# A fused dynamic convolution, rational MLP and SwiGLU kernel: weight decode and bounds moved, the convolution's taps laid innermost, a fixed order of work

## Chip, cores and metric

The kernel runs on one core of a Trainium2 chip. The metric is the device time of one execution in microseconds (us); lower is better. PE is TensorE, DVE VectorE, ACT ScalarE, POOL GpSimd, SP SyncE (which only issues DMAs here).

## What is computed

The input x has 2 x 4096 tokens of 192 channels, treated as 8192 tokens. Three layers follow one another; cut to what matters:

```python
w = softmax(weight_gen, axis=-1)                    # per token: 8 heads x 7 taps, 1e-09 added to the sum
x = einsum('bshk,bskhg->bshg', w, x_unf)            # causal window of 7 tokens, 24 channels per head
h = x @ w_in                                        # 192 -> 2048
P = a[0] + a[1] * h + a[2] * h2 + a[3] * h3
Q = 1.0 + np.abs(b[0]) * np.abs(h) + np.abs(b[1]) * h2
x = (P / (Q + 1e-6)) @ w_out                        # 2048 -> 192
xn = x / rms * rms_g
silu = g * (1.0 / (1.0 + np.exp(-g)))               # g = xn @ w_gate, 192 -> 1536
out = silu * (xn @ w_val) @ w_out                   # 1536 -> 192, a second w_out
```

The four weight matrices arrive as float64, everything else as float32.

## The kernel before

**Tiling.** A partition holds 64 tokens in a row. The work is cut into 32 blocks of 256 tokens (two per partition). In a block the 2048 hidden columns of the first MLP are four quads of 512, so there are 128 quads; the 1536 columns of the second are two halves of 768.

**A block.** The softmax over the taps (jobs "s", some for two or four blocks at once) runs on DVE, POOL and ACT. POOL multiplies x with each of the seven taps (L352, tile pt, taps outermost); the sum over taps is a reduction on DVE with a strided read (L361) or, for the first six blocks, six additions on POOL (L367, the rule ADDP). ACT takes the fp16 part (L371), POOL the rest (L375), and a transposing DMA on SP makes xt (L380). mm1 is, for each quad, four groups of five fp16 matmuls (L767) of the split weights w1A, w1B and w1C into the PSUM tile h, of which there are two. The rational function of a quad is then a chain over the engines: ACT squares h into tB (L777) and takes its scaled magnitude into tA (L781); DVE makes Q in tA ("q", L784); ACT takes logarithm and exponential of it, 1/Q in tC (L788, L791); DVE makes P in h (p1 and p2, L795, L799) and the fp16 product g1h (L804); ACT adds a constant to Q (qc, L807), POOL multiplies it with g1h (m, L810), DVE subtracts (d, L813) and POOL makes the fp16 rest g1l (L817). d is the last to read h, and so what frees it for the quad two further on. mm2 (L833 to L835) multiplies g1h and g1l with the split w_out into acc, of which there is one buffer. The RMS norm runs on ACT and POOL; its fp16 parts xn are written by ACT (L872) and POOL (L876), and a transposing DMA makes xnT (L881). mm3 makes gate and val (L767) in the PSUM tile gv, a single buffer; ACT's silu (L907) frees it for val, DVE's product (L912) for the next gate. mm4 (L921) multiplies in float32 with the second w_out, ACT copies out (L927) and SP stores.

**Weights.** Each of 20 pieces of the float64 weights is decoded to float32. ACT makes a mask in SBUF in three operations (L423, L425, L426: square, sign, relu), DVE assembles the bits in three (L445, L451, L454), all on SBUF. Then bounds are taken that set powers of two as scales: ACT squares each piece (L469), for w_in PE sums the squares with a matrix of ones (L472) into gv, and allmax (L155, L156) takes the maximum over partitions with a transpose on PE into gv. ACT and either POOL (L497) or DVE (L499) split each piece into fp16 parts.

**What sets the order.** Every operation is a job with an engine, a cost, its dependencies and the buffers that it takes. order() gives each job a due time, from the list TIMES for the first blocks and for the rest from a period T_SLOT of 9.8432 per quad and the offsets OFF, and a list scheduler in the kernel then writes the program, engine by engine. Each engine works its queue in order. All DMAs are on SP's queue.

## Time and profile before

| what | value |
|---|---|
| device time, median of 3 runs | 1412.8 us |
| lowest and highest | 1411.08 and 1414.57 us |
| the profiled execution: its span | 1411.8 us |
| another time of that execution | none is given; the span is used as its own time |
| PE busy | 1241.5 us, 88% |
| DVE busy | 1200.8 us, 85% |
| ACT busy | 1153.9 us, 82% |
| POOL busy | 1044.7 us, 74% |
| DMA, mean | 38 GB/s |

The busy times are of the whole span. Matmul records are pipelined and overlap, so a matmul's own mean is not what it adds to the time; the distance from one start to the next is.

### The profile page before, as it was taken

What the parts mean: (1) busy time and instruction counts of PE and PEld (TensorE: products, weight loads), DVE (VectorE), ACT (ScalarE), POOL (GpSimd) and SP (SyncE); (2) the same over time, 40 slices, a digit from 0 to 9 for tenths busy, and PEclk for the clock granted to TensorE, in tenths of its full rate; (3) what the DMA queues carried; (4) which work ended last, traced back from release to release, by engine and by line L of the source; (5) the groups of instructions that cost most, each with busy time, mean ns of one, the idle gap of its engine ahead of it and who ended that gap; (6) DMA issues with size and microseconds to landing.
All of it is one profiled execution on the core that took longest, in us unless ns stands there. A gap on an engine that the chain in (4) does not pass through costs nothing.

```text
span 1411.8 us, 26479 instructions
## 1 busy us (share of the span) xinstructions
PE 1241.5 (88%) x11026; PEld 1134.7 (80%) x11026; DVE 1200.8 (85%) x1018; ACT 1153.9 (82%) x1410; POOL 1044.7 (74%) x874
## 2 busy tenths in 40 slices
PE   1313488999999999999999999999999999999998
PEld 0212378889889988888889898898889898999997
DVE  5999998888988888888899888888888988888741
ACT  5777877888888888888888888888888888888862
POOL 2977797988777777788777777777877777777540
PEclk9657799999999999999999999999999999999999
DMA  7432233100100020000200010001000000000000
GB/s 200 143 96 70 57 85 78 51 22 18 58 15 16 12 61 18 21 18 18 61 18 16 15 57 13 21 18 60 18 18 21 13 21 13 15 16 18 18 12 18
DMA packets 70664, 54.19 MB, mean 38 GB/s; under 512 B 54034, under 2 KB 66194, under 8 KB 69648
## 3 DMA queue, kind: packets, MB, share of 16 engines
q1 hardware_dynamic: 70544, 52.51, 14.0%
q8 instruction: 86, 1.41, 0.4%
q14 instruction: 34, 0.28, 0.1%
HBM read 31.26 MB, written 6.29 MB: 27 GB/s over the span
## 4 chain that ended last, share of the span: by engine, by line
PE 37%; DVE 16%; ACT 14%; POOL 13%; issue 5%; DMA 4%; POOLq 0%; DVEq 0%; ACTq 0%
PE gv L767 15%; PE h L767 9%; PE acc L921 6%; POOL g1l L817 6%; DMA xnT<-xn 4%; DVE tA L784 3%; DVE g1h L804 3%; DVE h L799 3%; POOL tA L810 3%; POOL xn L876 2%; DVE gp L912 2%; ACT tC L791 2%; ACT tC L788 2%; ACT tA L807 2%; PE acc L835 2%
## 5 line engine op out<-in xcount | busy, mean ns | idle before, releaser
L810 POOL TENSOR_TENSOR tA<-tA,g1h 128x1024 f32<-128x1024 f32 x128 | 276.6, 2161 | 194.5 <-DVE g1h L804 174.0
L817 POOL TENSOR_TENSOR g1l<-tA,tC 128x1024 f16<-128x1024 f32 x128 | 306.8, 2409 | 52.7 <-DVE tA L813 32.5
L767 PE MATMUL h<-xt,w1A 128*128 128x256 f16 x1024 | 220.8, 278 | 86.4 <-DVE tA L813 68.2
L921 PE MATMUL acc<-wo,gp 128*128 128x192 f32 x1464 | 252.3, 327 | 1.5 <-ACT osb L927 1.4
L833 PE MATMUL acc<-wo1h,g1h 128*128 128x192 f16 x1008 | 248.0, 246 | 0.4 <-ACT y L840 0.4
L834 PE MATMUL acc<-wo1l,g1h 128*128 128x192 f16 x1008 | 248.0, 246 | 0.0
L835 PE MATMUL acc<-wo1h,g1l 128*128 128x192 f16 x1008 | 248.0, 246 | 0.0
L352 POOL TENSOR_TENSOR pt<-xc,wg 128x384 f32<-128x384 f32 x224 | 241.9, 1105 | 1.8
L921 PEld LDWEIGHTS acc<-wo,gp 128*128 128x128 f32 x1464 | 236.8, 191 | 3.0 <-ACT osb L927 1.7
L784 DVE SCALAR_TENSOR_TENSOR tA<-tB,cf,tA 128x1024 f32<-128x1024 f32 x128 | 201.8, 1577 | 32.9 <-ACT tA L781 32.9
L777 ACT ACTIVATE tB<-h 128x1024 f32<-128x1024 f32 x128 | 130.5, 1020 | 90.2 <-PE h L767 90.2
L767 PE MATMUL h<-xt,w1C 128*128 128x256 f16 x1024 | 200.2, 278 | 0.0
L813 DVE SCALAR_TENSOR_TENSOR tA<-h,cf,tA 128x1024 f32<-128x1024 f32 x128 | 163.7, 1279 | 41.8 <-POOL tA L810 41.8
L767 PE MATMUL gv<-xnT,w3gA 128*128 128x256 f16 x756 | 164.7, 275 | 33.1 <-DMA xnT<-xn 29.1
L795 DVE SCALAR_TENSOR_TENSOR h<-tB,cf,h 128x1024 f32<-128x1024 f32 x128 | 163.5, 1279 | 34.4 <-ACT tA L781 31.3
L767 PEld LDWEIGHTS <-w1A 128*128 128x128 f16 x1024 | 102.0, 100 | 95.9 <-DVE tA L813 42.6
L767 PE MATMUL gv<-xnT,w3vA 128*128 128x256 f16 x768 | 170.2, 273 | 6.1 <-ACT gp L907 6.1
L804 DVE SCALAR_TENSOR_TENSOR g1h<-h,cf,tC 128x1024 f16<-128x1024 f32 x128 | 163.6, 1278 | 12.0 <-ACT tC L791 3.4
L781 ACT ACTIVATE tA<-h,cf 128x1024 f32<-128x1024 f32 x128 | 142.0, 1110 | 35.2 <-PE h L767 19.1
L799 DVE SCALAR_TENSOR_TENSOR h<-tB,cf,h 128x1024 f32<-128x1024 f32 x128 | 163.9, 1281 | 1.3
L788 ACT ACTIVATE tC<-tA,cf 128x1024 f32<-128x1024 f32 x128 | 146.5, 1145 | 20.7 <-DVE tA L784 19.9
L912 DVE SCALAR_TENSOR_TENSOR gp<-gp,val_s,gv 128x1536 f32<-128x1536 f32 x64 | 115.8, 1810 | 51.5 <-PE gv L767 51.0
(215 smaller groups left out, 2844.4 us busy)
## 6 DMA issues: line engine op xcount, KB each, us to landing
xc<-in_x_dram SPq DMA_DIRECT2D x7, 1344.0 KB, 6.6
...
```

Of the source, the lines that this page charges most:

```text
L352: nc.gpsimd.tensor_tensor(out=pt_t[b][:, k].rearrange("p i (h g) -> p i h g", h=NH), in0=xc_t[k0][:, o0 + k:o0 + k + 2, :].rearrange("p i ...
L767: nc.tensor.matmul(out=dst, lhsT=w[:, fs], rhs=xt[:, :, c, :], start=(n == 0), stop=(n == 4))
L784: nc.vector.scalar_tensor_tensor(out=tA[q], in0=tB[q], scalar=cfb(q)[:, 1:2], in1=tA[q], op0=ALU.mult, op1=ALU.add)
L788: nc.scalar.activation(out=tC[q], in_=tA[q], func=ACTF.Ln, scale=float(2.0 ** -LNS), bias=cfb(q)[:, 8:9])
L799: nc.vector.scalar_tensor_tensor(out=h, in0=tB[q], scalar=cf[:, 5:6], in1=h, op0=ALU.mult, op1=ALU.add)
L804: nc.vector.scalar_tensor_tensor(out=g1h[q], in0=hps[q], scalar=cf[:, 3:4], in1=tC[q], op0=ALU.add, op1=ALU.mult)
L810: nc.gpsimd.tensor_tensor(out=tA[q], in0=tA[q], in1=g1h[q], op=ALU.mult)
L817: nc.gpsimd.tensor_tensor(out=g1l[q], in0=tA[q], in1=tC[q], op=ALU.mult)
L833: nc.tensor.matmul(out=acc[:, 0:D], lhsT=g1h[q][:, r, ts], rhs=wo1h[:, f, :], start=(f == 0), stop=False)
L834: nc.tensor.matmul(out=acc[:, 0:D], lhsT=g1h[q][:, r, ts], rhs=wo1l[:, f, :], start=False, stop=False)
L835: nc.tensor.matmul(out=acc[:, 0:D], lhsT=g1l[q][:, r, ts], rhs=wo1h[:, f, :], start=False, stop=(f == N1 - 1))
L921: nc.tensor.matmul(out=acc[:, 0:D], lhsT=gp[b, k][:, i // 2, i % 2, ts], rhs=wo2[:, f, :], start=(f == 0), stop=(f == N2 - 1))
```

## The change

- Decode: ACT makes one square per piece (L461 of the changed kernel). DVE assembles the bits in four operations (L478, L481, L484, L487), the fourth with the mask test in it, and the intermediate lies in PSUM: in two slots of a new tile dslot, or for w_in in an h buffer. Only the three pieces of the second w_out keep it in SBUF. A table VAR marks choices; it marks 13 of the 20 pieces with 1 under "way". The cost of a marked piece is that of three operations on ACT, with the fourth on no engine; the code tests for the value 2, so every piece gets the four operations on DVE.
- Bounds of w_in and of the first w_out: 50 float32 products of 128 columns with themselves on PE (L501, dec_g) into acc and a maximum over them, in place of ACT's squares and the matrix of ones. allmax uses an h or acc buffer, and gv is opened once the decoding no longer needs dslot.
- Convolution: the tile pt has the taps innermost, so POOL writes with a step of 28 bytes and DVE's reduction reads contiguously. The sum over taps is on POOL for the blocks 0, 1 and 17 and on DVE for the others. For the blocks 0 and 1 the taps are not scaled with x's scale; ACT scales the sum instead (L397).
- Rational function: for 19 of the 128 quads q is an ACT operation (L812) and an addition on POOL (L816); qc then falls away.
- Several operations on single columns are merged; the DMAs that spread the packed thirds of the weights (w1C, w3gC) are jobs of their own.
- Order: a list RANK of some 4,000 numbers gives the order of all jobs, in place of due times and list scheduler, and PICK the buffer for five of them.

The diff, cut to its core:

```diff
-    SQB = 2
+    SQB = 1
...
+    dec_ctx = tc.tile_pool(name="ps_d", bufs=1, space=PSUM)
+    dslot = dec_ctx.__enter__().tile([128, 2, 768], FP32, name="dslot")
...
+    VAR = {('way', ('in', (0, 1))): 1, ('way', ('in', (2, 3))): 1, ('way', ('in', (4, 5))): 1, ('way', ('in', (6,))):
+           1, ('ms', ('in', (0, 1))): 1, ('ms', ('in', (4, 5))): 1, ('ms', ('in', (6,))): 1, ('way', ('o1', (0,))): 1,
...
+           109): 1, ('qp', 122): 1, ('qp', 127): 1}
...
+    def pick(g):
+        return VAR.get(g, 0)
...
         def s_eps():
             sm = sm_t[c]
+            if c < NFREE:
+                nc.gpsimd.tensor_single_scalar(out=sm[:, 0:n], in_=sm[:, 0:n], scalar=1e-9, op=ALU.add)
+                return
             nc.gpsimd.tensor_scalar(out=sm[:, 0:n], in0=sm[:, 0:n], scalar1=1e-9, scalar2=iv_t[cset(c)],
                                     op0=ALU.add, op1=ALU.mult)
...
-                pt_t[b] = at_p.tile([128, KS, 2, D], FP32, tag="pt", name="pt")
+                pt_t[b] = at_p.tile([128, 2, D, KS], FP32, tag="pt", name="pt")
             nc.gpsimd.tensor_tensor(
-                out=pt_t[b][:, k].rearrange("p i (h g) -> p i h g", h=NH),
+                out=pt_t[b][:, :, :, k].rearrange("p i (h g) -> p i h g", h=NH),
...
         def add(i):
+            if not pick(("ap", b)):
+                if i < 3:
+                    add_v(i - 1)
...
+                add_p(i)
+        def add_v(i):
             if i == 0:
                 ac_t[b] = at_p.tile([128, 2, D], FP32, tag="ac", name="ac")
-            nc.vector.tensor_reduce(out=ac_t[b][:, i, :], in_=pt_t[b][:, :, i, :].rearrange("p k d -> p d k"),
+            nc.vector.tensor_reduce(out=ac_t[b][:, i, :], in_=pt_t[b][:, i],
                                     axis=AX.X, op=ALU.add)
...
         def add_p(k):
             if k == 1:
                 ac_t[b] = at_p.tile([128, 2, D], FP32, tag="ac", name="ac")
-            nc.gpsimd.tensor_tensor(out=ac_t[b], in0=pt_t[b][:, 0] if k == 1 else ac_t[b], in1=pt_t[b][:, k], op=ALU.add)
+            nc.gpsimd.tensor_tensor(out=ac_t[b], in0=pt_t[b][:, :, :, 0] if k == 1 else ac_t[b], in1=pt_t[b][:, :, :, k], op=ALU.add)
...
+            if c < NFREE:
+                nc.scalar.activation(out=ac_t[b], in_=ac_t[b], func=ACTF.Copy, scale=sx_t[0])
             nc.scalar.activation(out=hl_t[b][:, :, 0:D], in_=ac_t[b], func=ACTF.Copy)
...
+                dec_t[key] = (wo2[:, key[1] * OW:(key[1] + 1) * OW, :].rearrange("p k f -> p (k f)") if key[0] == "o2"
+                              else lent_dec(P_3.index(key[1:])) if key[0] == "g" else st_p.tile([128, 768], FP32, tag="dec", name="dec", bufs=DECB))
+            sq = us[key] if way == 2 else dec_t[key][:, 0:width]
             nc.scalar.activation(out=sq, in_=raw[:, 0:width, 1].bitcast(FP32), func=ACTF.Square, scale=32768.0)
-            if way:
+            if way == 2:
                 nc.scalar.activation(out=sq, in_=sq, func=ACTF.Sign, bias=thr)
-                nc.scalar.activation(out=sq, in_=sq, func=ACTF.Relu,
-                                     scale=float(np.uint32(0x3FFFFFF8).view(np.float32)) if way == 2 else 1.0)
...
+    def dec_b(unit, items, part):
+        way = pick(("way", unit))
+        if part == 4 and way == 2:
+            return
...
+            dst, u = dec_t[key][:, 0:width], us[key].bitcast(U32)
+            if part < 4:
+                H, L = raw_t[key][:, 0:width, 1], raw_t[key][:, 0:width, 0]
...
-                    out=u, in0=H, scalar=0xC0000000, in1=u, op0=ALU.bitwise_and, op1=ALU.bitwise_or)
+                    out=dst.bitcast(U32) if way == 2 else u, in0=H, scalar=0xC0000000, in1=u, op0=ALU.bitwise_and, op1=ALU.bitwise_or)
...
                 nc.vector.scalar_tensor_tensor(
-                    out=dst, in0=sq, scalar=1.4, in1=dst, op0=ALU.is_ge, op1=ALU.mult)
...
+                    out=dst, in0=dst, scalar=1.4, in1=us[key], op0=ALU.is_ge, op1=ALU.mult)
...
-                cs = gv[:, 0].rearrange("p i t -> p (i t)")
-                nc.tensor.matmul(out=cs[:, 0:width], lhsT=ones, rhs=sq, start=(key[1:] == P0[0]), stop=(key[1:] == P0[-1]))
+            nc.scalar.activation(out=us[key], in_=dec_t[key][:, 0:width], func=ACTF.Square, accum_out=sumcol)
+    def dec_g(items, i):
+        nm = items[0][0][0]
+        if nm not in gram:
+            gram[nm] = ps_a.tile([128, 4, 128], FP32, tag="acc", name="acc")
+        cuts = [(key, a) for key, width, dst, sumcol in items for a in range(0, width, 128)]
+        for j, (key, a) in enumerate(cuts):
+            w = dec_t[key][:, a:a + 128]
+            nc.tensor.matmul(out=gram[nm][:, i], lhsT=w, rhs=w, start=(j == 0), stop=(j == len(cuts) - 1))
...
-    def dve_q(q):
-        nc.vector.scalar_tensor_tensor(out=tA[q], in0=tB[q], scalar=cfb(q)[:, 1:2], in1=tA[q], op0=ALU.mult, op1=ALU.add)
+    def act_ty(q):
+        tC[q] = tp_p.tile([128, 4, 256], FP32, tag="tC", name="tC")
+        if pick(("qp", q)):
+            nc.scalar.activation(out=tC[q], in_=tB[q], func=ACTF.Identity, scale=cfb(q)[:, 1:2], bias=cfb(q)[:, 2:3])
+    def add_q(q):
+        if pick(("qp", q)):
+            nc.gpsimd.tensor_tensor(out=tA[q], in0=tA[q], in1=tC[q], op=ALU.add)
+        else:
+            nc.vector.scalar_tensor_tensor(out=tA[q], in0=tB[q], scalar=cfb(q)[:, 1:2], in1=tA[q], op0=ALU.mult, op1=ALU.add)
...
+        if pick(("qp", q)):
+            nc.scalar.activation(out=tC[q], in_=tA[q], func=ACTF.Ln, scale=float(2.0 ** -LNS))
...
+        if pick(("qp", q)):
+            return
...
+    def gv_open():
+        dec_ctx.__exit__(None, None, None)
+        late["gv"] = ctx.enter_context(tc.tile_pool(name="ps_g", bufs=1, space=PSUM)).tile([128, NJ, 2, 256], FP32, name="gv")
...
-    def ADDP(b):
-        return b < 6
+    RANK = [7, 14, 24, 38, 42, 33, 34, 37, 40, 47, 63, 39, 41, 43, 44, 51, 46, 49, 52, 53, 57, 76, 54, 59, 60, 62, 72,
...
+    PICK = {('mm2', 31, 0, 0): "h", ('mm4', 30, 0, 0): "h", ('mm4', 29, 1, 0): "h", ('mm4', 31, 0, 0): "h", ('mm4', 31, 1, 0): "h"}
...
+        out, tab = [], "e"
+        for i in sorted(range(len(keys)), key=lambda i: RANK[i]):
```

**Where instructions move.** Names such as wdec, dec and sq are the decoded piece and its mask, raw, wo_120 and w3vC places where the float64 words lie, cf the coefficients. First, ACT at the decoding of w_in. Before:

```order
L423 ACTIVATE wdec<-raw 128x512
L425 ACTIVATE wdec<-wdec,thr 128x512
L426 ACTIVATE wdec<-wdec 128x512
L469 ACTIVATE wdec<-wdec 128x512 x2
L319 ACTIVATE wg<-wg 128x112
L423 ACTIVATE wdec<-raw 128x512
L425 ACTIVATE wdec<-wdec,thr 128x512
L426 ACTIVATE wdec<-wdec 128x512
L423 ACTIVATE wdec<-raw 128x256
L425 ACTIVATE wdec<-wdec,thr 128x256
L426 ACTIVATE wdec<-wdec 128x256
```

Now, from the start of ACT's queue:

```order
L1392 ACT_TABLE_LOAD
L461 ACTIVATE dec<-raw 128x768
L461 ACTIVATE wdec<-raw 128x512
L334 ACTIVATE wg<-wg 128x112 x2
L461 ACTIVATE wdec<-raw 128x512 x4
L461 ACTIVATE wdec<-raw 128x256
L461 ACTIVATE wdec<-raw 128x512
L515 ACTIVATE w1A_102<-wdec,s_in 128x512
```

The operations L425 and L426 are gone, and the squares L469; what was L423 stands alone as L461.

Second, DVE up to the first d (L813 before, L851 now). Before:

```order
L784 SCALAR_TENSOR_TENSOR tA<-tB,cf_135,tA 128x1024
L451 SCALAR_TENSOR_TENSOR w3vB<-raw,w3vB 128x768
L309 TENSOR_REDUCE mx<-wg 128x32
L795 SCALAR_TENSOR_TENSOR h<-tB,cf_135,h 128x1024 x2
L799 SCALAR_TENSOR_TENSOR h<-tB,cf_135,h 128x1024 x2
L804 SCALAR_TENSOR_TENSOR g1h<-h,cf_135,tC 128x1024
L454 SCALAR_TENSOR_TENSOR w3vB<-raw,w3vB 128x768
L445 SCALAR_TENSOR_TENSOR w3vC<-wo_120,sq 128x768
L804 SCALAR_TENSOR_TENSOR g1h<-h,cf_135,tC 128x1024
L451 SCALAR_TENSOR_TENSOR w3vC<-wo_120,w3vC 128x768
L813 SCALAR_TENSOR_TENSOR tA<-h,cf_135,tA 128x1024
```

Now:

```order
L831 SCALAR_TENSOR_TENSOR h<-tB,cf_133,h 128x1024
L835 SCALAR_TENSOR_TENSOR h<-tB,cf_133,h 128x1024
L831 SCALAR_TENSOR_TENSOR h<-tB,cf_133,h 128x1024
L350 RECIPROCAL sm<-sm 128x32
L481 SCALAR_TENSOR_TENSOR dslot<-raw,dslot 128x768
L835 SCALAR_TENSOR_TENSOR h<-tB,cf_133,h 128x1024
L840 SCALAR_TENSOR_TENSOR g1h<-h,cf_133,tC 128x1024
L478 TENSOR_SCALAR dslot<-wo_120 128x768
L484 SCALAR_TENSOR_TENSOR dslot<-raw,dslot 128x768
L481 SCALAR_TENSOR_TENSOR dslot<-wo_120,dslot 128x768
L851 SCALAR_TENSOR_TENSOR tA<-h,cf_133,tA 128x1024
```

Both have decode operations of later weights between the rational function's; q (L784) is not among them now, and the decode operations write dslot instead of the weight's own place.

Third, POOL at the end of block 18's norm, where xn is written (y_9183 and y_9133 are the tile of the normed block). Before:

```order
L810 TENSOR_TENSOR tA<-tA,g1h 128x1024
L860 TENSOR_SCALAR ms<-ssq 128x2
L861 TENSOR_TENSOR u<-r 128x2
L862 TENSOR_TENSOR u<-u,ms 128x2
L863 TENSOR_SCALAR u<-u,cf_136 128x2
L864 TENSOR_TENSOR r<-r,u 128x2
L817 TENSOR_TENSOR g1l<-tA,tC 128x1024
L876 TENSOR_TENSOR xn<-y_9183,xn 128x2x128
L876 TENSOR_TENSOR xn<-y_9183,xn 128x2x64
L352 TENSOR_TENSOR pt<-xc,wg 128x384 x2
```

Now:

```order
L848 TENSOR_TENSOR tA<-tA,g1h 128x1024
L898 TENSOR_SCALAR ms<-ssq 128x2
L899 TENSOR_TENSOR u<-r 128x2
L900 TENSOR_TENSOR u<-u,ms 128x2
L901 TENSOR_SCALAR u<-u,cf_134 128x2
L902 TENSOR_TENSOR r<-r,u 128x2
L914 TENSOR_TENSOR xn<-y_9133,xn 128x2x128
L914 TENSOR_TENSOR xn<-y_9133,xn 128x2x64
L855 TENSOR_TENSOR g1l<-tA,tC 128x1024
```

xn (L876, now L914) stood behind g1l (L817, now L855), and now stands ahead of it.

## Rows read from the trace of the kernel before

**Rows 1.** The page: busy us, share of the span and instructions of each engine.
```profile
PE 1241.5 (88%) x11026; PEld 1134.7 (80%) x11026; DVE 1200.8 (85%) x1018; ACT 1153.9 (82%) x1410; POOL 1044.7 (74%) x874
```
**Rows 2.** Windows: stretch, its length, busy us (instructions) by engine; clock, DMA.
```profile
core 0: us, PE busy (x) PEld busy (x) DVE busy (x) ACT busy (x) POOL busy (x), PEclk, DMA share, GB/s
...
70.00:105.00 35.00, 4.88 (x24) 3.39 (x25) 31.75 (x28) 26.86 (x34) 27.22 (x18) 0.51 0.36 93
175.00:210.00 35.00, 27.99 (x252) 24.39 (x253) 33.51 (x26) 26.69 (x34) 32.74 (x26) 0.90 0.26 70
500.00:700.00 200.00, 193.88 (x1746) 178.76 (x1745) 174.72 (x131) 170.65 (x206) 154.22 (x128) 1.00 0.12 32
```
**Rows 3.** Chain that ended last: start us, us, engine, tile and line, matmuls.
```profile
308.87 2.18 PE h L767 x20
...
653.43 2.34 PE gv L767 x20
...
731.47 2.34 PE gv L767 x20
...
1240.19 3.90 PE acc L921 x24
```
**Rows 4.** Timeline of PE: first and last of 36 matmuls; start us, own us.
```profile
237.12 0.25 PE L833 MATMUL acc<-wo1h,g1h 128*128 128x192 f16 x1
...
240.00 0.25 PE L835 MATMUL acc<-wo1h,g1l 128*128 128x192 f16 x1
```
**Rows 5.** Waits of PE: us in all, number, longest.
```profile
PE h L767 <- DVE tA L813: 68.2, 17, 32.3
```
**Rows 6.** Timeline of DVE: the first and the eighth product.
```profile
198.81 1.80 DVE L912 SCALAR_TENSOR_TENSOR gp<-gp,val_s,gv 128x1536 f32<-128x1536 f32 x1
...
333.36 1.82 DVE L912 SCALAR_TENSOR_TENSOR gp<-gp,val_s,gv 128x1536 f32<-128x1536 f32 x1 [0.76 <-PE gv L767]
```
**Rows 7.** Groups of PE, 500 to 1300 us: busy, mean ns | idle before, releasers.
```profile
L767 PE MATMUL h<-xt,w1A 128*128 128x256 f16 x656 | 138.8, 273 | 5.3 <-DVE tA L813 5.3
L767 PE MATMUL gv<-xnT,w3vA 128*128 128x256 f16 x492 | 110.2, 273 | 2.8 <-ACT gp L907 2.8
L767 PE MATMUL gv<-xnT,w3gA 128*128 128x256 f16 x492 | 105.9, 272 | 12.6 <-DMA xnT<-xn 10.5 <-DVE gp L912 2.0
```
**Rows 8.** Groups of the whole run, shapes apart: busy us, mean ns | idle before.
```profile
L810 POOL TENSOR_TENSOR tA<-tA,g1h 128x1024 f32<-128x1024 f32 x128 | 276.6, 2161 | 194.5 <-DVE g1h L804 174.0 <-ACT tC L791 19.8 <-DVE srow_v L620 0.5
...
L352 POOL TENSOR_TENSOR pt<-xc,wg 128x384 f32<-128x384 f32 x224 | 241.9, 1105 | 1.8
...
L784 DVE SCALAR_TENSOR_TENSOR tA<-tB,cf,tA 128x1024 f32<-128x1024 f32 x128 | 201.8, 1577 | 32.9 <-ACT tA L781 32.9
...
L804 DVE SCALAR_TENSOR_TENSOR g1h<-h,cf,tC 128x1024 f16<-128x1024 f32 x128 | 163.6, 1278 | 12.0 <-ACT tC L791 3.4 <-DVE h L799 1.8 <-ACT tA L807 0.5
...
L361 DVE TENSOR_REDUCE ac<-pt 128x192 f32<-128x1344 f32 x52 | 131.1, 2522 | 0.0
...
L367 POOL TENSOR_TENSOR ac<-ac,pt 128x384 f32<-128x384 f32 x30 | 39.3, 1309 | 1.3
...
L445 DVE SCALAR_TENSOR_TENSOR wdec<-raw,wdec 128x512 uint32<-128x512 uint32 x6 | 4.8, 818 | 4.8 <-ACT wdec L426 4.8
...
L256 DVE TENSOR_SCALAR tt<-tt 128x1 f32<-128x1 f32 x14 | 2.8, 236 | 0.0
```
**Rows 9.** Timeline of DVE: single operations; start us, us, idle before in brackets.
```profile
9.84 1.55 DVE L225 TENSOR_REDUCE xmx<-xc 128x1 f32<-128x1344 f32 x1 [7.69 <-DMA xc<-in_x_dram]
...
79.93 2.39 DVE L451 SCALAR_TENSOR_TENSOR w3vA<-raw,w3vA 128x768 uint32<-128x768 uint32 x1
...
87.04 0.95 DVE L451 SCALAR_TENSOR_TENSOR w3vB<-raw,w3vB 128x768 uint32<-128x768 uint32 x1
```
**Rows 10.** Timeline of POOL and ACT at a block's xn.
```profile
646.26 2.37 POOL L817 TENSOR_TENSOR g1l<-tA,tC 128x1024 f16<-128x1024 f32 x1
...
647.27 0.52 ACT L872 ACTIVATE xn<-y 128x384 f16<-128x384 f32 x1
...
648.58 2.04 POOL L876 TENSOR_TENSOR xn<-y,xn 128x256 f16<-128x256 f32 x2
```

More of the change, by code (lines that the diff above doesn't have):

```diff
@@ new lines, in prep_jobs @@
+            decs = sum((q[3] for q in pcs), [])
+            prev = ends
+            if nm in ("g", "v"):
+                job(("dc", u), "A", ca(width) + 0.4 * len(p), lambda it=it: dec_c(it),
+                    prev, use=slot + decs)
+            elif nm != "o2":
+                job(("G", u), "T", 0.0018 * width + 0.1, lambda it=sum((q[0] for q in pcs), []), i=by[nm].index(u): dec_g(it, i),
+                    prev + [first_g.get(nm)], use=decs + [("acc", nm)], new=() if nm in first_g else [("acc", nm)])
+                first_g.setdefault(nm, ("G", u))
@@ L1159 @@
         if k == 0:
[L1160 removed]
+            job(("xa", k), "V", 1.0, lambda k=k: x_all(k), [("xm", i) for i in cols], new=[("h", ("xa", k))])
         else:
```

475 lines of the change are left out of this document (154 added, 321 removed), and 344 rows, old and new, of tables (RANK, TIMES, VAR).

## Prediction

> **What bounds the kernel now.** I read the page's busy line first: PE is busy 88% of the span, DVE 85%, ACT 82%, POOL 74% [rows 1]. No engine is full, so I read by stretch. From 500 to 700 us PE is busy 193.88 of 200 us at a granted clock of 1.00; from 70 to 105 us it is busy 4.88, and there DVE holds 31.75 of 35 us; from 175 to 210 us DVE has 33.51 and POOL 32.74 [rows 2]. So the start belongs to DVE (the decoding of the weights and the first quads of the rational function), the rest to PE.
>
> To size the start I need PE's bare work. A quad of mm1 is 20 matmuls in 2.18 us, 0.109 each; a half of mm4 is 24 in 3.90 us [rows 3]. From the first to the last of 36 matmuls of mm2 are 35 steps in 2.88 us, 0.0823 each [rows 4]. mm1 is 128 quads x 2.18 = 279 us, gate and val 128 x 30 x 0.109 = 419, mm4 64 x 3.90 = 250, mm2 32 x 96 x 0.0823 = 253: 1200 us in all. The span is 1411.8, so 212 us are lost. The view of PE's waits names the largest loss: PE waited 68.2 us in 17 waits for the operation d, which frees an h buffer, once for 32.3 us [rows 5]. The first product of DVE starts at 198.81 and the eighth at 333.36 [rows 6]. By the order, PE has by the first of them done 10 quads (21.8), 14 pieces of mm2 at 12 matmuls (13.8) and 6 of gate or val at 10 (6.5), 42 us: 157 are lost. By the eighth it has done 165 and lost 168. The other 44 us lie in the 28 later blocks and the end. From 500 to 1300 us PE's named waits are 5.3 (h for d), 2.8 (val for the silu), 10.5 (gate for the transposed xn) and 2.0 (gate for the product), 20.6 us [rows 7].
>
> **The start, on DVE.** I added up DVE's instructions by the order up to the first product, each at its price: 180.4 us before, against the 198.81 + 1.80 where that product ends, so 20 us of idling. The same sum for the change:
>
> - q: 10 before, 2 now, the others an addition on POOL. 8 x 1.58 [rows 8] = -12.6. POOL gets 8 x 2.16 = 17.3 for it, and loses 6 additions of taps (6 x 1.3 = 7.9) [rows 8] and two splits; it has 7.8 us idle in the 35 from 70 us, but 2.3 in the 35 from 175 us [rows 2], so this cover is thin at the end. ACT's part replaces another one for one.
> - Decode: 60 operations before, 80 now (part 4 runs on DVE for every piece; 7 of 20 pieces were to be so by the table). The old price has two values: the same 768-wide operation takes 2.39 us in one place and 0.95 in another [rows 9]. I take about their middle, 1.6, and for 512 columns the mean of a row, 0.82 [rows 8]: 39 x 1.6 + 18 x 0.82 + 3 x 0.45 = 79 us. Now 68 of the 80 work in PSUM, which nothing in the trace shows for this operation. Lower end: the undisturbed 0.95. Upper end: 1.6 as in SBUF, which would be 30 us more in all. I take 0.97: the 1024-wide operations that read h in PSUM average 1.28 [rows 8] and 1.28 x 768/1024 is 0.96. For 512 and 256 columns I take a little over a half and a quarter of 1.28, 0.68 and 0.4. So 40 x 0.97 + 24 x 0.68 + 4 x 0.4 = 57, and the 12 of w_out2 that stay in SBUF 12 x 1.6 = 19: 76, which is -3.
> - Sums over the taps: two more on DVE. The strided one takes 2.52 [rows 8], a contiguous read of the same 1344 elements 1.55 [rows 9]; these are both ends, and I take 1.55, since taps innermost are contiguous: +3.1.
> - Splits, 5 before, 7 now; the two are 512 wide, two thirds of 1.6 each: +2.1. Single-column operations, 92 before, 75 now, at 0.236 [rows 8]: -3.6.
>
> Sum -14. PE has done 2 us less by then (40 against 42), so the loss shrinks by 12. At the eighth product the sums differ by 16.9 with equal PE work, but 7 us of that are single-column operations that only come later, and the product there waited 0.76 for PE itself [rows 6]: I take another -3. The other edits of the start I cost at nothing, and this is their cover. ACT loses 40 mask operations and 11 squares and gains two scalings of the sums; it waits for DVE there. [...] SP now issues a piece of w_out ahead of the conv weights, and x behind the first w_in pieces, so DVE begins with decoding where it stood idle for 7.69 us until x came [rows 9]; if the w_out piece lands no sooner than x did, nothing is won, and I count nothing. The DMAs that spread w_in's packed halves are a job of their own now, and their wait holds SP and what is queued there; three of these groups stand ahead of the first block's transpose before, two now, so I count nothing for them either.
>
> Multiplications of the taps: on POOL they now write with a step of 28 bytes. Nothing in the trace writes so. Lower end: 1.105, as today [rows 8]; upper: times 2.52/1.55, the price of DVE's strided read, 1.80. I take 1.105, because POOL already needs 2.1 to 2.9 ns per element, more than the 1.88 of DVE's strided read. At 1.80 POOL would be busy 35 of the 39 us of a block (worked out below): still cover.
>
> The trace has 1.31 us for an addition of taps on POOL [rows 8], read contiguously. [...]
>
> **The steady part.** The chain comes to PE's gate through xnT at 653.43 and, two blocks later, at 731.47, so a block takes 39.0 us [rows 3]. xnT comes from POOL: g1l from 646.26 for 2.37 us, then xn from 648.58 for 2.04, then the transposing DMA; ACT's part was ready at 647.27 + 0.52 [rows 10]. In 30 of 32 blocks of the order xn stands behind that g1l, in the change in 12 of 32: it leaves up to 1.4 us earlier. Matmul work between the end of val and the next gate, which is the time that DVE has for its product, was 2.0 to 3.0 us in every second case, now at least 3.9 and mostly 6.1. Between gate and val it was 3.0 to 4.1 in most, is now mostly 6.1, with 12 of 64 at 2.0 to 2.2. So of the 20.6 us I take off 7.5 (xnT) and 5 (product, silu, d): 12.5 in 800 us, for the 1080 us after the eighth product times 1.27 is -16. DVE's sum over the whole kernel falls by 75 us (19 q, 52 contiguous reductions), which takes the edge off its waits; the 12 short gaps cost new ones, +2. So -14.
>
> **Sum.** 1411.8 - 12 - 3 - 14 = 1382.8 by the profiled execution. The profile gives no other time of that execution; the median of the runs is 1.0 above its span, so **1384**.
>
> **Rivals.**
>
> *The steady waits stay.* The silu is bound to ACT and the matmul work between mm2's end and the first gate is 11.5 us in both orders, so the xn chain could end as late as now. Only the start gains: 1411.8 - 15 + 1 = 1397. For: the waits are small and spread. Against: xn's earlier place.
>
> *The order was made with other durations.* The table marks 13 pieces as having no part 4 on DVE, the code gives it to all: 13 x 0.97 = 12.6 us on DVE, on the engine that sets the start, that the order puts nowhere. Because the queues run in order, an operation that comes late holds all behind it. Then the start's 15 are nearly eaten and part of the steady gain with them: 1404 to 1412. Against: my sum already counts the 80 operations.
>
> *POOL becomes the bound (slower).* From 500 to 700 us POOL is busy 154.22 of 200 [rows 2], 30.1 per block of 39.0, of which the 7 multiplications are 7.7 and the rest 22.4. Their new write step decides from (39.0 - 22.4)/7 = 2.37 us on. At 2.5 POOL needs 39.9 per block: 28 blocks x 0.9 = 25 us more, the 14 multiplications of the first two blocks take 20 us longer, half of it beside the decoding: 1411.8 + 25 + 10 - 15 + 1 = 1433. For: no row prices such a write. Against: that is 2.3 times today's price, and DVE's read went from 1.55 to 2.52, 1.6 times.
> [...]
>
> *Better than the sum.* All of the 20.6 us go, and DVE's 20 us of idling in the start shrink by a third as ACT is freed from the masks: 1384 - 8 - 7 = 1369, down to 1362.
>
> **Chances.** The sum (1370 to 1396) 0.50; better 0.10; steady waits stay 0.15; order made with other durations 0.12, 0.07 of it inside no change; POOL as the bound and other slips 0.13. What a measurement can tell from no change is 0.3%, 4.2 us: 1408.6 to 1417. So faster 0.80, same 0.07, slower 0.13. The range 1362 to 1410 leaves out the slower rival, the upper end of the order's and the tail below.
>
> **What would show it.** The reduction over taps near 1.55 us; the multiplication near 1.1 (over 2.37 makes the slower rival true); decode operations with dslot near 0.97 (at 1.6 the start gains nothing); the first product at about 186 instead of 198.81; PE's named waits from 500 to 1300 us near 10 instead of 20.6, xnT's first. If the first product comes at 186 and the waits stay at 20, the first rival was right; if it comes after 195, the second.

## The result

The changed kernel takes 1373.7 us (median of 4 runs, 1372.22 to 1374.41), the kernel before 1413.7 in the same comparison: the ratio is 0.9715, 95% interval 0.9697 to 0.9734. That is 40 us faster, where 28.8 were forecast (1384); the time lies in the range. The profiled execution's span is 1372.3 us.

The page of the changed kernel, busy us by engine, and windows of its trace (columns as in [rows 2]):

```profile
PE 1254.0 (91%) x11113; PEld 1154.3 (84%) x11113; DVE 1140.7 (83%) x1006; ACT 1113.4 (81%) x1357; POOL 1045.4 (76%) x873
```

```profile
70.00:105.00 35.00, 10.92 (x57) 7.06 (x55) 33.17 (x43) 29.20 (x35) 29.06 (x20) 0.68 0.22 61
175.00:210.00 35.00, 34.27 (x284) 30.55 (x282) 28.26 (x26) 28.04 (x36) 24.41 (x22) 0.95 0.27 78
500.00:700.00 200.00, 197.41 (x1788) 183.48 (x1786) 167.74 (x131) 175.40 (x214) 164.11 (x139) 1.00 0.08 18
```

Against [rows 1] DVE lost 60 us of busy time and ACT 41; POOL is as busy as before. Against [rows 2] DVE still fills the stretch from 70 us on; from 175 us on it no longer does, and PE is at work there. From 500 to 700 us PE has 3.5 us more of 200.

The largest waits of PE over the whole run, and the first and the eighth product in the timeline of DVE:

```profile
PE h L793 <- DVE tA L851: 44.2, 15, 13.2
PE acc L501 <- DVE wdec L487: 26.4, 3, 20.8
PE acc L501 <- DVE dec L487: 12.6, 2, 8.4
```

```profile
179.28 1.81 DVE L954 SCALAR_TENSOR_TENSOR gp<-gp,val_s,gv 128x1536 f32<-128x1536 f32 x1 [4.17 <-PE gv L793]
...
310.02 1.80 DVE L954 SCALAR_TENSOR_TENSOR gp<-gp,val_s,gv 128x1536 f32<-128x1536 f32 x1
```

The wait for d is 44.2 us where it was 68.2 [rows 5]; the two waits on L501 are the Gram products waiting for decoded pieces, all ahead of the first quad of mm1. That quad starts at 67.2 us, directly behind the last of them, and its transposed x had landed at 53.2; so the 12.6 us may have held it back. That the Gram products cost the start nothing, as the working took it, is not shown. The first product starts 19.5 us sooner than in [rows 6], the eighth 23.3 us. PE's groups from 500 to 1300 us, which answer to [rows 7]:

```profile
L793 PE MATMUL h<-xt,w1A 128*128 128x256 f16 x672 | 142.1, 273 | 2.4 <-DVE tA L851 2.2
L793 PE MATMUL gv<-xnT,w3gA 128*128 128x256 f16 x504 | 104.5, 273 | 1.7 <-DMA xnT<-xn 1.0 <-DVE gp L954 0.3
L793 PE MATMUL gv<-xnT,w3vA 128*128 128x256 f16 x496 | 102.8, 273 | 0.9 <-ACT gp L949 0.8
```

The four waits that the prediction named are 2.2 + 1.0 + 0.3 + 0.8 = 4.3 us, where they were 20.6. Two others have come in their place, PE's waits for an acc buffer in the same stretch:

```profile
PE acc L963 <- ACT osb L969: 2.8, 6, 0.9
...
PE acc L871 <- ACT y L878: 0.8, 2, 0.4
```

With them it is 7.9 us, 12.7 fewer than before. With PE's bare work at each point (42.1 us at the first product before and 40.1 now, 165.2 at the eighth, 1200 in all), the loss went from 156.7 to 139.2 up to the first product, from 11.5 to 5.6 up to the eighth, and from 43.6 to 27.5 behind it: 17.5 + 5.9 + 16.1 = 39.5 us.

The prices, in groups of the whole run, shapes apart:

```profile
L370 POOL TENSOR_TENSOR pt<-xc,wg 128x384 f32<-128x384 f32 x224 | 219.8, 1029 | 3.7 <-DMA xc<-in_x_dram 2.7
...
L818 DVE SCALAR_TENSOR_TENSOR tA<-tB,cf,tA 128x1024 f32<-128x1024 f32 x109 | 180.3, 1654 | 25.9 <-ACT tA L807 21.5 <-ACT tB L803 4.2
...
L386 DVE TENSOR_REDUCE ac<-pt 128x192 f32<-128x1344 f32 x58 | 87.6, 1543 | 0.4 <-POOL pt L370 0.4
...
L816 POOL TENSOR_TENSOR tA<-tA,tC 128x1024 f32<-128x1024 f32 x19 | 46.3, 2436 | 14.5 <-ACT tC L812 13.5 <-ACT tA L807 0.9
...
L392 POOL TENSOR_TENSOR ac<-ac,pt 128x384 f32<-128x384 f32 x15 | 18.7, 1248 | 1.0
...
L487 DVE SCALAR_TENSOR_TENSOR dec<-dec,dslot 128x768 f32<-128x768 f32 x7 | 6.6, 947 | 0.3
...
L481 DVE SCALAR_TENSOR_TENSOR sq<-raw,sq 128x768 uint32<-128x768 uint32 x3 | 5.5, 1822 | 0.1
```

The reduction over taps takes 1.54 us as forecast, POOL's multiplication with its write step of 28 bytes 1.03, a decode operation with its intermediate in PSUM 0.95, and the dearest of the four that stayed in SBUF 1.82; the twelve of the second w_out there average 1.55.

### The profile page after: what moved, and what is told of

Its sections match the earlier page's. It is cut to its first block, busy times and chain, and to the rows that moved or that the text cites. A ratio compares the mean times of both kernels' runs of the same rounds, so it can differ in the third digit from the quotient of the medians.

```text
span 1372.3 us, 26538 instructions
## 1 busy us (share of the span) xinstructions
PE 1254.0 (91%) x11113; PEld 1154.3 (84%) x11113; DVE 1140.7 (83%) x1006; ACT 1113.4 (81%) x1357; POOL 1045.4 (76%) x873
## 4 chain that ended last, share of the span: by engine, by line
PE 55%; DVE 18%; ACT 9%; POOL 9%; issue 5%; DMA 3%; SPq 0%; POOLq 0%; DVEq 0%; ACTq 0%
PE gv L793 20%; PE h L793 12%; PE acc L963 10%; DVE tA L818 4%; PE acc L871 4%; PE acc L873 4%; PE acc L872 4%; POOL tA L848 3%; DVE g1h L840 2%; DVE tA L851 2%; POOL g1l L855 2%; DVE h L835 2%; ACT tA L807 1%; POOL pt L370 1%; ACT tB L803 1%
## 5 line engine op out<-in xcount | busy, mean ns | idle before, releaser
L855 POOL TENSOR_TENSOR g1l<-tA,tC 128x1024 f16<-128x1024 f32 x128 | 318.7, 2492 | 77.3 <-DVE tA L851 69.0
L848 POOL TENSOR_TENSOR tA<-tA,g1h 128x1024 f32<-128x1024 f32 x128 | 282.4, 2207 | 111.9 <-DVE g1h L840 67.7
L793 PE MATMUL h<-xt,w1A 128*128 128x256 f16 x1024 | 222.8, 280 | 45.0 <-DVE tA L851 44.2
L963 PE MATMUL acc<-wo,gp 128*128 128x192 f32 x1440 | 246.5, 327 | 3.0 <-ACT osb L969 2.8
L851 DVE SCALAR_TENSOR_TENSOR tA<-h,cf,tA 128x1024 f32<-128x1024 f32 x128 | 163.9, 1281 | 91.3 <-POOL tA L848 91.2
L963 PEld LDWEIGHTS acc<-wo,gp 128*128 128x128 f32 x1440 | 232.4, 190 | 6.2 <-ACT osb L969 5.0
L370 POOL TENSOR_TENSOR pt<-xc,wg 128x384 f32<-128x384 f32 x224 | 219.8, 1029 | 3.7 <-DMA xc<-in_x_dram 2.7
L818 DVE SCALAR_TENSOR_TENSOR tA<-tB,cf,tA 128x1024 f32<-128x1024 f32 x109 | 180.3, 1654 | 25.9 <-ACT tA L807 21.5
L840 DVE SCALAR_TENSOR_TENSOR g1h<-h,cf,tC 128x1024 f16<-128x1024 f32 x128 | 163.8, 1280 | 14.6 <-ACT tC L827 8.0
L793 PE MATMUL gv<-xnT,w3vA 128*128 128x256 f16 x768 | 160.4, 274 | 11.6 <-ACT gp L949 11.5
L824 ACT ACTIVATE tC<-tA,cf 128x1024 f32<-128x1024 f32 x109 | 125.0, 1147 | 52.9 <-DVE tA L818 51.4
L793 PE MATMUL gv<-xnT,w3gA 128*128 128x256 f16 x756 | 157.8, 274 | 4.9 <-DVE gp L954 3.0
```

The source lines that it names most:

```text
L370: nc.gpsimd.tensor_tensor(out=pt_t[b][:, :, :, k].rearrange("p i (h g) -> p i h g", h=NH), in0=xc_t[k0][:, o0 + k:o0 + k + 2, :].rearrange ...
L793: nc.tensor.matmul(out=dst, lhsT=w[:, fs], rhs=xt[:, :, c, :], start=(n == 0), stop=(n == 4))
L818: nc.vector.scalar_tensor_tensor(out=tA[q], in0=tB[q], scalar=cfb(q)[:, 1:2], in1=tA[q], op0=ALU.mult, op1=ALU.add)
L840: nc.vector.scalar_tensor_tensor(out=g1h[q], in0=hps[q], scalar=cf[:, 3:4], in1=tC[q], op0=ALU.add, op1=ALU.mult)
L848: nc.gpsimd.tensor_tensor(out=tA[q], in0=tA[q], in1=g1h[q], op=ALU.mult)
L851: nc.vector.scalar_tensor_tensor(out=tA[q], in0=hps[q], scalar=cfb(q)[:, 3:4], in1=tA[q], op0=ALU.add, op1=ALU.subtract)
```

## The experiments

The changed kernel differs from the old one in its operations and in its order. The first question was which of the two gave the 40 us; the working ahead had given the start to DVE's operations and the steady part to the order. Each time is given with its ratio to the kernel before, run beside it; the changed kernel stands at 0.9715. Where a run is called slower than the changed kernel by some us, that is a difference of medians; by the ratios it comes out up to 2 us higher. Differences of 4 to 6 us (e4, e9, e10, e12) are little above what such runs can tell apart (the four of e12 lie 5.1 us apart).

### e1: the old operations in the new order

```diff
-        times, want = iter(TIMES), []
-        for k in keys:
...
+        want = list(WANT)
```

WANT holds, for each job of the old kernel, its place in RANK's order.

> The kernel before with its own operations and engines (mask on ACT, decode on SBUF, strided sums over the taps, q on DVE, bounds from ACT's squares), written in the order of the changed kernel; PE's queue is that of the changed kernel. Theory of the sum: the steady part is a matter of the order (xn ahead of g1l, longer gaps), the start of DVE's work. So the steady gain of 14 to 17 us comes here, most of the start's 23 us does not: 1393 to 1402 us, the first product within 6 us of 198.8, PE's wait for xnT from 500 to 1300 us under 3 us. Rival, the durations: the order fits only the new durations of DVE; with 2 us more DVE work per block its gaps turn into waits for d and for the product, and the time is 1409 to 1420 us.

Measured: 1477.3 us, ratio 1.0445 (1.0427 to 1.0464). Both theories fell short: the new order alone makes the kernel 64 us slower. The first product is at 228.5 us. PE's waits up to there, of this kernel:

```profile
PE h L767 <- DVE tA L813: 56.5, 7, 17.0
PE gv L155 <- DVE mloco L605: 42.6, 1, 42.6
PE gv L472 <- ACT wdec L469: 32.1, 2, 30.3
```

and DVE's largest:

```profile
DVE dec L445 <- ACT sq L426: 23.6, 3, 20.7
```

The transposes for the bounds (L155) stand at the place that the new order gives them; with the old masks and squares on ACT PE waits 42.6 us for one of them, and everything behind it in PE's queue waits too. DVE is busy 152.6 of the 228.5 us, so here the start is not bound by its work. Of the 61 us by which the span is longer than that of before, 40 have gathered by the eighth product and 22 come behind it. In the steady part a block takes 39.6 us (950.5 us for the 24 blocks from the eighth product to the 56th), where the old order had 39.0 and the changed kernel 38.2; PE's wait for d from 500 to 1300 us is 16.0, as the rival has it, where it was 5.3.

### e2: the new operations in the old order

The mirror image: the old list scheduler with each job's place in the old program.

```diff
-        for i in sorted(range(len(keys)), key=lambda i: RANK[i]):
...
+        want = list(WANT)
```

> The changed kernel's operations and engines in the order of the kernel before; PE's queue, the Gram products apart, is that of before, and xn stands behind g1l in 30 of 32 blocks again. Theory of the sum: the start's gain comes (DVE's sum up to the first product is 12.8 us below that of before), the steady gain does not, because xn's place is the old one: 1390 to 1400 us, the first product at 180 to 188 us, PE's wait for xnT from 500 to 1300 us near 10 us. Rival, the durations: DVE's 75 us less do the work wherever they fall, so most of the steady gain comes as well: 1375 to 1386 us. Second rival, the order is all: 1405 us or more.

Measured: 1440.1 us, ratio 1.0186 (1.0167 to 1.0204): the order-is-all rival. The first product comes at 197.9 us, 1 us sooner than before, though DVE is busy 157.3 us up to there, 17 less than before. PE's waits up to 200 us:

```profile
PE h L793 <- DVE tA L851: 36.4, 6, 17.3
...
PE h L170 <- DVE mloco L632: 24.2, 1, 24.2
```

Here too the bound of the first w_out (L170) blocks PE's queue, 24.2 us, where the changed kernel waits 0.8 for it. That this wait is what holds the first product is argued from its size and place, not shown by a run of its own. So neither half is worth anything alone, in the places that these two runs give to its jobs: +64 and +27 us, and together -40. The effects do not add.

### e3 and e11: one duration in both orders

The cleanest operation to test this on is the sum over taps, since the layout of pt changes no queue. e3 takes it back in the changed kernel, e11 makes it in the old one.

```diff
-                pt_t[b] = at_p.tile([128, 2, D, KS], FP32, tag="pt", name="pt")
+                pt_t[b] = at_p.tile([128, KS, 2, D], FP32, tag="pt", name="pt")
...
-            nc.vector.tensor_reduce(out=ac_t[b][:, i, :], in_=pt_t[b][:, i],
+            nc.vector.tensor_reduce(out=ac_t[b][:, i, :], in_=pt_t[b][:, :, i, :].rearrange("p k d -> p d k"),
```

> The changed kernel with the taps outermost again in the tile pt, order and engines unchanged. Theory of the sum: the 58 reductions go from 1.54 to 2.52 us, DVE has 57 us more, 2 of them ahead of the first product and 8 more up to the eighth; the first product is 2 us later, the steady waits for d and for the product grow by 2 to 8 us: 1378 to 1386 us. POOL's multiplication goes back from 1.03 to 1.10 us. Rival, cover: in the steady part DVE's idle time takes the 1.9 us per block, and nothing is seen beyond the start: 1374 to 1377 us.

Measured: 1398.8 us, ratio 0.9898 (0.9881 to 0.9916), 25 us slower than the changed kernel and more than either theory gave. The reduction went to 2.51 us. The first product is at 180.3, 1 us later; nearly all of the loss is behind the eighth (311.9). PE's waits of this kernel, 500 to 1300 us:

```profile
PE h L793 <- DVE tA L851: 9.9, 14, 1.6
PE acc L963 <- ACT osb L969: 5.1, 6, 2.1
PE gv L793 <- DMA xnT<-xn: 3.7, 4, 1.0
```

A block takes 39.1 us instead of 38.2: of 1.9 us more on DVE 0.9 reaches the end, most of it as waits for d, for ACT's copy and for xnT. That is the 39.0 of the kernel before: with the strided sum the new order has no steady gain left. The windows of the changed kernel and of e3 show it in PE's column, the first:

```profile
500.00:1300.00 800.00, 791.45 (x7205) 735.97 (x7203) 675.76 (x521) 702.01 (x850) 643.11 (x536) 1.00 0.10 23
```

```profile
500.00:1300.00 800.00, 778.19 (x7051) 719.68 (x7048) 704.72 (x516) 689.69 (x833) 638.80 (x533) 1.00 0.10 23
```

e11 is the same edit, the other way round, in the kernel before.

> The kernel before with the taps innermost as the only edit: 52 reductions of DVE go from 2.52 to 1.54 us, POOL's multiplication stays near 1.1 and its additions of the first six blocks rise a little. In the changed order the same edit was worth 25 us (e3). Additive theory, DVE's time is worth the same in any order: 20 to 25 us faster, 1389 to 1394 us. Rival, a matched order: in the order of before the engines' waits come from ACT and POOL (tA, two buffers), DVE waits there for ACT anyway, and the edit brings less than 5 us: 1408 to 1417 us.

Measured: 1412.8 us, ratio 0.9995 (0.9983 to 1.0006): nothing, with the reduction at 1.54 us as in the changed kernel. The windows of before and of e11, and DVE's largest waits, 500 to 1300 us. Before:

```profile
500.00:1300.00 800.00, 779.24 (x7078) 720.94 (x7077) 705.41 (x520) 690.13 (x828) 614.34 (x516) 1.00 0.10 25
```

```profile
DVE tA L784 <- ACT tA L781: 28.3, 12, 3.1
DVE tA L813 <- POOL tA L810: 23.1, 22, 1.4
```

e11:

```profile
500.00:1300.00 800.00, 779.59 (x7085) 721.54 (x7085) 670.56 (x521) 691.57 (x830) 614.30 (x516) 1.00 0.10 25
```

```profile
DVE tA L813 <- POOL tA L810: 57.4, 60, 2.0
```

DVE's busy time (third) fell by 34.9 us, and its wait for POOL's m rose by 34.3. In the old order the operation behind the reduction is d, which waits for POOL's m, so the time saved is spent there; PE's column did not move. One such place, before and in e11:

```profile
712.89 2.54 DVE L361 TENSOR_REDUCE ac<-pt 128x192 f32<-128x1344 f32 x1
715.36 1.27 DVE L813 SCALAR_TENSOR_TENSOR tA<-h,cf,tA 128x1024 f32<-128x1024 f32 x1
```

```profile
712.85 1.54 DVE L361 TENSOR_REDUCE ac<-pt 128x192 f32<-128x1344 f32 x1
715.27 1.28 DVE L813 SCALAR_TENSOR_TENSOR tA<-h,cf,tA 128x1024 f32<-128x1024 f32 x1 [0.89 <-POOL tA L810]
```

In this stretch 39 of the 41 reductions stand directly ahead of a d; these 39 d waited 1.0 us in all before and 35.4 in e11, 0.91 each. In the place shown d starts 2.4 to 2.5 us after the reduction has begun, long or short: the long reduction just filled the time until m. In the changed order the two reductions of a block stand together, and 15 of 21 pairs stand directly ahead of a d. These d wait 4.3 us in all in the changed kernel and not at all in e3: two contiguous reductions nearly fill the time until m, two strided ones go beyond it and make d late. There the same saving is worth 25 us.

### e7: the same operation shorter still

```diff
-            nc.vector.tensor_reduce(out=ac_t[b][:, i, :], in_=pt_t[b][:, i],
+            nc.vector.tensor_reduce(out=ac_t[b][:, i, :], in_=pt_t[b][:, i, :, 0:4],
```

> The changed kernel, but DVE's reduction sums only four of the seven taps (a part of the sum is left out), which should bring it from 1.54 to about 0.95 us; nothing else changes. e3 made the same 58 operations 0.97 us longer and the kernel 25 us slower, 0.89 us per block. Theory, DVE's time counts in both directions: 1.2 us less per block give 0.5 us per block back, 1355 to 1362 us. Rival, a matched order: the order leaves no gap for work that comes late, but work that is early waits at the next operation in the queue; PE with its 37.5 us per block is nearly full: 1370 to 1375 us.

Measured: 1372.7 us, ratio 0.9717 (0.9692 to 0.9742), the changed kernel's own time, with the reduction at 0.94 us. The rival holds: 0.97 us more of this operation costs 25 us, 0.6 us less gives nothing. Its window, and DVE's largest wait from 500 to 1300 us in the changed kernel and in e7:

```profile
500.00:1300.00 800.00, 791.39 (x7202) 735.72 (x7201) 652.77 (x522) 702.74 (x848) 641.47 (x536) 1.00 0.10 23
```

```profile
DVE tA L851 <- POOL tA L848: 72.7, 56, 3.5
```

```profile
DVE tA L851 <- POOL tA L848: 91.7, 62, 3.4
```

Of the 23 us that DVE is less busy, 19 turn up as its wait for m, 13.6 of them at the 15 d behind the reductions. PE is busy 791 of the 800 us in both, so at most 8.6 us were to be had in this stretch. Two things keep the gain at nothing, the wait for m and a PE that is nearly full; e7 does not part them. For longer operations the order has no room.

### e5 and e6: the place of xn

The prediction's steady part rested on POOL's xn ahead of g1l. e5 moves it back behind in 15 blocks of the changed kernel, e6 moves it ahead in 30 blocks of the old one. Only POOL's queue changes (in e6 one magnitude on ACT, in e5 one output DMA changes its place too).

```diff
-    RANK = [7, 14, 24, 38, 42, 33, 34, 37, 40, 47, 63, 39, 41, 43, 44, 51, 46, 49, 52, 53, 57, 76, 54, 59, 60, 62, 72,
...
```

In place of this list stands the same one, with the number of ("xl", b) just above that of the g1l behind it. In e6 the same is done by WANT.

> The changed kernel with one thing of its order undone: in the 15 blocks where POOL's xn stands directly ahead of a g1l, it is moved behind that g1l, as in the order of before; the other engines' queues stay. Theory of the prediction's steady part (the place of xn): most of its 10 us come back, 1380 to 1384 us, PE's wait for xnT from 500 to 1300 us grows from 1.0 to 5 us or more. Rival, a matched order: what counts is that the whole fits DVE's durations, and a single place of POOL, which has 20% of idle time, is worth less than 3 us: 1372 to 1376 us.

Measured: 1384.0 us, ratio 0.9799 (0.9776 to 0.9823), 10 us slower than the changed kernel, as the prediction's term says; of the 10.5 us by which the span is longer, 2.9 are there by the eighth product and 7.7 come behind it. PE's wait, 500 to 1300 us, was 1.0 and is

```profile
PE gv L793 <- DMA xnT<-xn: 7.6, 7, 1.9
```

> The kernel before with one thing of its order changed: in the 30 blocks where POOL's xn stands directly behind a g1l, it is moved ahead of that g1l; the queues of PE, DVE and SP stay. Theory of the prediction's steady part: PE's wait for xnT from 500 to 1300 us falls from 10.5 to 3 us or less and the time by about 10 us: 1400 to 1406 us. Rival, a matched order: the POOL waits for ACT's part of xn, g1l comes 2 us later and mm2 or d with it; the loss turns up elsewhere: 1410 to 1425 us.

Measured: 1471.1 us, ratio 1.0427 (1.0384 to 1.0470): 58 us slower. PE's wait for xnT fell to 3.2 us, exactly as meant, and yet a block takes 41.1 us. PE's largest waits, 500 to 1300 us, in e6:

```profile
PE acc L921 <- ACT osb L927: 34.0, 20, 2.8
PE h L767 <- DVE tA L813: 9.9, 16, 1.5
PE gv L767 <- DMA xnT<-xn: 3.2, 10, 0.5
```

and what ACT waits for there:

```profile
ACT tA L781 <- POOL g1l L817: 67.7, 22, 4.5
```

Before, ACT's magnitude waited for g1l 8.7 us in that stretch. The chain that these waits suggest: xn, put ahead, waits on POOL for ACT's part (30.2 us, 19 waits); g1l comes that much and xn's 2 us later; g1l is the last to read tA, of which there are two; ACT's next magnitude needs one and stands still, 67.7 us; ACT's copies of mm4's result stand behind it in ACT's queue, and PE, with one acc, waits for those. In the changed order, where xn stands directly ahead of a g1l in 15 blocks, ACT waits only 2.3 us for g1l in this stretch.

### e8: q back on DVE

```diff
-           109): 1, ('qp', 122): 1, ('qp', 127): 1}
```

All 19 entries "qp" of the table are taken out; its last line stands for them.

> The changed kernel with q of all 128 quads on DVE, as before, in the changed order; ACT makes the constant's addition for the 19 quads again and POOL loses 19 additions of 2.44 us. Theory of the sum, term q of the start: 8 operations of 1.6 to 1.8 us come back ahead of the first product and one more up to the eighth, 13 to 16 us; the other 10 lie beside PE's work: 1386 to 1392 us. Rival, POOL's gain covers it: POOL, which holds 29 of 35 us from 70 us on, loses as much, so the first product is at most 5 us later: 1373 to 1379 us. Second rival, a matched order: each of the 10 later ones also makes the next waits late by most of its length: 1395 us or more.

Measured: 1400.6 us, ratio 0.9916 (0.9891 to 0.9940), 27 us slower: the second rival. The timeline of DVE, first product:

```profile
190.48 1.82 DVE L946 SCALAR_TENSOR_TENSOR gp<-gp,val_s,gv 128x1536 f32<-128x1536 f32 x1 [1.33 <-PE gv L785]
```

It is 11.2 us later, against 12.6 in the sum, so the term q of the start was right. The eighth is 12.3 later, and the other 15 us come behind it, where the other 10 quads lie: 1.5 us each in the mean, with q at 1.62. They do not all cost the same: against the changed kernel the delay is 15.0 us from the eleventh to the twentieth product, 21.5 from the thirtieth to the fiftieth, no more after the quad 109, and 27.7 at the last, behind the quads 122 and 127. The sum had not priced these.

### e9: half the decoding back in SBUF

```diff
-            t = dslot[:, len(nslot) % 2]
+            t = (dslot[:, 1] if len(nslot) % 2 else
+                 st_p.tile([128, 768], FP32, tag="sqd", name="sqd", bufs=1))
```

> The changed kernel with every second 768-wide piece of the decoding kept in SBUF instead of PSUM (the first of the two slots of dslot becomes an SBUF tile); order and engines unchanged, so both places stand side by side in one trace. Theory of the sum, term decode: about 20 operations go from 0.95 to 1.4 to 1.7 us where POOL works beside them, DVE gets 9 to 15 us more ahead of the first product, and the first product comes that much later: 1382 to 1390 us. Rival: the price in SBUF comes from the old order, in which POOL worked beside the decoding; here it is near 0.95 for most, and the time stays within 4 us: 1370 to 1378 us.

Measured: 1377.7 us, ratio 0.9752 (0.9732 to 0.9772); the first product is at 182.4, 3.1 us later. Groups of this kernel, SBUF (sqd) beside PSUM (dslot):

```profile
L488 DVE SCALAR_TENSOR_TENSOR dec<-dec,sqd 128x768 f32<-128x768 f32 x3 | 5.0, 1658 | 0.0
...
L488 DVE SCALAR_TENSOR_TENSOR dec<-dec,dslot 128x768 f32<-128x768 f32 x4 | 3.8, 947 | 0.2
...
L482 DVE SCALAR_TENSOR_TENSOR sqd<-raw,sqd 128x768 uint32<-128x768 uint32 x3 | 2.8, 950 | 0.0
```

The 20 operations on sqd average 1.14 us (22.8 us in all, single ones from 0.55 to 3.08), so they add 3.8 us to DVE, and 3.1 of these reach the first product. The rival was nearer: in this order SBUF is not 1.6 in the mean.

### e4 and e10: the marks taken as they are costed

The table marks 14 units of decoding, 17 pieces, not 13 as the text ahead has it, and the code ignores the marks. e4 follows them.

```diff
-        way = pick(("way", u))
+        way = 2 * pick(("way", u))
...
-        way = pick(("way", unit))
+        way = 2 * pick(("way", unit))
```

> The changed kernel with the table's marks taken as they are costed: for the marked 17 pieces ACT makes the mask with three operations and DVE's fourth operation falls away. Theory of the sum: DVE, which sets the start, loses 17 operations (7 x 0.68 + 8 x 0.95 + 2 x 1.5 = 15 us), ACT gets 34 of 0.6 to 0.9 us (27 us) and has 75 us idle up to the first product; the first product comes 6 to 12 us sooner: 1362 to 1369 us. Rival: DVE's first decode operation now waits for three operations of ACT in place of one, and ACT's added work stands ahead of the first quads' squares in its queue; the first product comes no sooner or up to 5 us later: 1372 to 1380 us.

Measured: 1378.0 us, ratio 0.9746 (0.9729 to 0.9763). The rival holds: DVE has 17 operations less and ACT 34 more, and yet the first product comes at 185.0, 5.7 us later. DVE's waits up to 185 us:

```profile
DVE dslot L475 <- ACT dslot L464: 7.9, 4, 2.7
DVE dslot L475 <- DMA wg<-in_weight_gen_dram: 5.9, 1, 5.9
DVE h L475 <- ACT h L464: 5.7, 4, 2.0
```

In the changed kernel DVE does not wait for ACT's square, because only its fourth operation needs it (no wait for L461 is among DVE's up to 185 us). With the mask first DVE starts each piece late.

e10 leaves w_in's pieces as they are.

```diff
+        way = 2 * pick(("way", u)) if u[0] != "in" else 0
```

> The changed kernel with the marks taken as costed, but not for w_in: 10 pieces of the first w_out, gate, val and the second w_out get their masks from three operations of ACT, and DVE's fourth falls away. e4 did it for w_in too and its first product came 5.7 us later, with DVE waiting 5.7 us for ACT's masks of w_in and 11 us for those of dslot. Theory that w_in's masks at the very start did the harm: DVE loses 10 operations (10.6 us) and the first product comes 2 to 8 us sooner than in the changed kernel: 1365 to 1372 us. Rival, any mask of three operations in this order holds DVE's queue: 1374 to 1380 us.

Measured: 1379.8 us, ratio 0.9767 (0.9747 to 0.9787), first product at 186.9. The rival holds: the masks of the later pieces do the harm too, DVE waits 13.7 us for them.

### e12: more q on POOL

```diff
-           109): 1, ('qp', 122): 1, ('qp', 127): 1}
+           109): 1, ('qp', 122): 1, ('qp', 127): 1, ('qp', 2): 1, ('qp', 7): 1, ('qp', 10): 1, ('qp', 11): 1}
```

> The changed kernel with q of four more of the early quads (2, 7, 10 and 11) as ACT's operation and POOL's addition. e8 showed that taking the 19 quads back costs 27 us, 11 of them ahead of the first product. Theory of the sum: two more q leave DVE ahead of the first product and two up to the eighth, 3 to 6 us sooner: 1367 to 1371 us. Rival, POOL is at its end there (29 of 35 us from 70 us on): its additions of 2.4 us hold m and g1l of the same quads, and the time is 1374 to 1382 us.

Measured: 1378.4 us, ratio 0.9763 (0.9736 to 0.9790). The first product comes at 178.2, 1.1 us sooner, the eighth at 314.0, 4.0 later. Two quads helped up to the first product. The harm comes with the quads 10 and 11: their additions lie at 195.5 and 204.2 us, and there the lead turns, from 1.1 us at the second product to 4.4 late at the third. (They were not tried without the other two.) So the table's choice of quads is part of the match as well, and no kernel of the twelve that does all the work is faster than the changed one.

## Why the prediction was right, and where its reasons were not

**What bounds the kernel**: right. The start is DVE's: its busy time up to the first product fell from 174.2 to 154.9 us, 19.3, and the product moved by 19.5. The rest is PE's: it is busy 791 of 800 us in the steady part now. But DVE sets the start only where the order fits: in e2 it has 17 us less to do and the product moves by 1.

**q at the start** (-12.6): right. The operation took 1.83 us there in the mean: the two of the ten that had POOL idle took 1.27 and 1.28, the eight beside a busy POOL 1.41 to 2.66. So the saving in DVE's own time was 15.6 us. e8 puts it back at 11.2 us at the first product; there q takes 1.29 and not 1.83.

**Decode** (-3, bounds to +27): right in the price, 0.95 where 0.97 was taken. It names 13 marked pieces where the table has 17, so by the table 3 of the 20 and not 7 had the fourth part; the 80 operations that it counted are those that ran. The sum of rows gives 81.0 us before and 75.0 now, -6. e9 says that the PSUM price is part of it: 1.14 in SBUF.

**Sums over the taps at the start** (+3.1): 3.1. **Splits and single-column operations** (+2.1 and -3.6): +0.2 and +0.8; the mean of one row was a poor price for the mixture, and the two misses partly cancel. (17 operations at 0.236 are 4.0, not 3.6; the slip is 0.4 us.)

**The start in all** (-12 and -3): -17.5 and -5.9. The direction and the place are right, the size is 8.4 us too small. Up to the first product the miss is 5.5, and DVE's rows give it: q at 1.83 instead of 1.58 makes 3.0, decoding 3, splits 1.9, operations of the softmax and of x's bound that the working left out 2.2, less 4.4 for the single-column ones, together 5.7.

**The steady part** (-14): -16.1. The waits went as said: the four named ones fell by 16.3 us in the 800, 9.5 of it xnT (7.5 were forecast), two new ones cost 3.6, and 12.7 remain of a forecast 12.5. (1080/800 is 1.35, not 1.27, so by its own terms the working should have had -15.) What it had incomplete is the reason. The term for xn's place is borne out by e5 in the changed order (6.6 us of wait, 7.7 us of time). The sentence that DVE's 75 us less "takes the edge off its waits" put nothing on the reductions, and that is the step that failed: in this order they are worth 25 us (e3), 22 of them behind the eighth product, and the ten later q 15 (e8). These and xn's 7.7 add up to 45, nearly three times the steady gain of 16, because they are not terms of a sum. The reductions' edit is worth nothing in the old order (e11), and xn's place costs 58 us there (e6); the q alone were not tried in it. The working took each price as a property of the edit; it is a property of the edit in its queue.

**First rival, the waits stay**: fell, 7.9 us with the two new ones instead of 20.6. With xn behind g1l again (e5) the one for xnT comes back to 7.6.

**Second rival, the order was made with other durations**: fell. It counted 13 pieces where the table marks 17. With the marks taken as costed the kernel is slower (e4, e10). But what it feared is real: e1, e3 and e8 show what the order does with operations that are longer than its own or on another engine, up to 64 us.

**Third rival, POOL by its writes** (from 2.37 us on): fell, 1.03 us; in e3 the contiguous write of the same order takes 0.99. The write with a step of 28 bytes takes 4% more, in this order (1.029 against 0.987) and in that of before (1.147 in e11 against 1.105). The additions of taps, with one of two inputs read with that step, took 1.248 us against 1.058 without it (e3), 18% more, and 1.516 against 1.309 in the old order (e11), 16%.

**What stays open**: why a block takes 39.5 us in e2, with less work on DVE than in the kernel before and PE's old queue. Its trace shows more waiting for xnT (14.6 us instead of 10.5 from 500 to 1300 us, once 5.6); that these come from the few quads with q on POOL in a queue that has no place for them was not tried by itself. Nor were the Gram products for the bounds, the merged single-column operations and the DMA jobs of their own: what each of them is worth is not shown.
